# Operands of the blend in buffers of their own, loaded in the last gated block; loads of b on GpSimd's queue

## The chip, the cores and the metric

The kernel runs on one core of one Trainium2 chip. The metric is the device time of one execution in microseconds; the times given are medians over several executions, with the lowest and the highest beside them. All durations are read from one profiled execution of each kernel.

## What is computed

A linear attention with a decaying state feeds two feed-forward layers; every matrix product is in fp32.

```python
x = attention(q, k, v)                    # 3072 tokens x 512
a, b = x @ w1, x @ w2                     # 512 -> 1024, the "gated" products
h = a * b @ w3                            # 1024 -> 1024
x = h @ w_out                             # 1024 -> 512
h = x @ w_in                              # 512 -> 2048
g = h * (1 / (1 + exp(-1.702 * h)))
out = g @ w_out2                          # 2048 -> 512
```

The kernel multiplies `w3` by `w_out` once, on the chip, and calls the product the mixed weights, so `a * b` goes straight to 512 features.

## The kernel before, in words

TensorE multiplies in a reduced format, so each fp32 operand is **split** into a high part (ScalarE casts, `split` at L261) and a residue (DVE subtracts, `residue` at L162), and each product is made of three matmuls (`mm3`, L246 to L248: high by high, high weight by residue, residue weight by high). The order of the instructions on each engine is the order of the program; each engine waits in that order.

The stages are: attention, with preparation of weights in its gaps; **gated products** over six blocks of 512 tokens in the order 0, 2, 4, 1, 3, 5; **mixing**, the product of `w3` and `w_out`, which runs within the third of these blocks; the **blend**, which multiplies `a * b` by the mixed weights; then `Expand` and `contract` for the last layer.

From mixing on the products are made by a scheme of seven products in place of eight (P1 to P7 in the order of `blends`: P1, P5, P6, P2, P7, P3, P4) on pairs of blocks. Blocks 0, 2, 4 (`gate_first`) store `a * b` to the DRAM tensor `hd`. Blocks 1, 3, 5 (`gate_second`) load back what was stored (`load_b`, tile `h` of two buffers in pool `xs`) and form five further operands `g[:, 0:5]` from it: DVE and GpSimd subtract (L1021, L1024, L1025, L1026), and GpSimd stores the 1280 KB tile `g` into `hd` (L1027). Each block has eight gates (`t` from 0 to 7) of 24 matmuls in two PSUM banks out of six, and two gates make one `g`, so a block has four pairs `k`. A b tile is released by the sum L1026 that reads it last. In the last block `opening(t)` also loads the first mixed weights `wm` and the operand of turn 0 (`load_h`, L796).

The blend has 21 turns, seven products for each of three pairs of blocks. Turn `n` needs one operand of 1 MB from `hd` (tile `l`, four tags `l0` to `l3` by `n % 4`, 8 KB per partition each): it is loaded by SyncE, called SP here (`load_turn`, three turns ahead from turn 1 on), cast by ScalarE into a tile `h` of two buffers, and replaced by its residue on DVE (`split_h`), then multiplied in 24 matmuls with one of the mixed weights. P1, P5 and P6 are copied out of PSUM by ScalarE into tiles `s` (`copied`, L852); the turn's copies stand in the program behind the split of the next turn. A bank that holds P1 is accumulated on by P6 at turn 2.

Tiles live in pools. Pools on the left side of the on-chip memory are stacked in the order in which they are opened: `big` (weights of the gates), then `b1` (mixing; closed when the eight mixed rows are done), then `b2` (tiles `st`, `b12`, an unused `gap` of 4 KB, and two `g` of 10 KB), and, after the gated stage, `c` in the same place (the blend: `l2`, `l3`, `l0`, `l1`, then `o`, `h`, `s`). A pool's size is settled once the whole program is written, and a tag gets its place in the pool by its first request. With `reuse_waits="tile"` the first user of a tile waits until all earlier tiles that lay at that place have been read for the last time, stores to DRAM included. The operand of turn 1 is loaded in two halves into tiles of the pool `prep`, in the seventh gate of the last block (`t == KF - 2`); turns 2 and 3 are loaded at the start of `blend`, with three loads of `wm` between them.

Of the kernel before, what the change touches and what calls it, by code (L numbers as in the profile page):

```python
# [8 lines left out]
F32R = mybir.dt.float32r  # L9
# [7 lines left out]
P = 128  # L17
# [4 lines left out]
TB = 512  # L22
NB = NT // TB
CPB = TB // P
KD, KF, KG = DM // P, DF // P, DG // P
ALPHA = 1.702
R_BUFS = 5
# [10 lines left out]
NM = KF // 2  # L38
ORDER = (0, 2, 4, 1, 3, 5)
# [4 lines left out]
def tile_kernel(  # L44
# [14 lines left out]
    nc = tc.nc  # L59
    first, second, third = (ctx.enter_context(ExitStack()) for _ in range(3))  # L60
# [226 lines left out]
    def h_tile():  # L287
        return xs.tile([P, 2, TB], F32, tag="h", bufs=2, name="h")
# [504 lines left out]
    def load_h(n, a, b, t):  # L793
        i, name = blends[n]
        lo2.setdefault(n, []).append((a, b, t))
        nc.sync.dma_start(t.bitcast(F32), hd[i][:, a:b, RIGHT[name]])  # L796
# [13 lines left out]
    def split_wm(n):  # L810
        hi, lo = wm[blends[n][1]]
        split(hi, lo, lo.bitcast(F32))

    def load_wm(n):
        name = blends[n][1]
        wm[name] = wtile("wg")
        nc.sync.dma_start(wm[name][1].bitcast(F32), sm[PART[name]].rearrange("p k c -> p (k c)"))

    def opening(t):
        if t in range(1, 5):  # L820
            load_wm(t - 1)
        if t == 1:
            x = spare.tile([P, 7, TB], F32R, tag="ope", name="h0")
            hi2[0] = x[:, NM:]
            load_h(0, 0, NM, x[:, :NM])
        if t == KF - 2:
            for k in (0, 2):
                load_h(1, k, k + 2, prep.tile([P, 2, TB], F32R, tag="r", bufs=R_BUFS, name="h1"))
        if t in (3, 4, 5):
            split_h(0, t - 3, t - 2, hi2[0][:, t - 3 : t - 2])  # L830
        if t == 6:
            hi2["k3"] = prep.tile([P, TB], F32R, tag="x", bufs=6, name="h3")
            split_h(0, 3, 4, hi2["k3"].rearrange("p (a t) -> p a t", a=1))
        if t in (4, 6):
            split_wm(t // 2 - 2)

    def blend(p, ps, todo):
        ws = {}

        def tile(kind, bufs):  # L840
            return p.tile([P, NM, TB], F32R, tag=kind, bufs=bufs, name=kind)

        def load_turn(n):
            if n < len(blends):
                load_h(n, 0, NM, ls.pop(n) if n in ls else tile(f"l{n % 4}", 1))

        def value():
            return p.tile([P, TB], F32, tag="s", bufs=8, name="s")

        def copied(ps):  # L850
            t = ready.pop() if ready else value()
            nc.scalar.copy(t, ps)  # L852
            return t

        def store(i, e, t):
            nc.gpsimd.dma_start(yd[i][:, e], t)

        ls = {n: tile(f"l{n % 4}", 1) for n in range(2, 6)}
        load_turn(2)
        for n in range(4, 7):  # L860
            load_wm(n)
        load_turn(3)
        held = [p.tile([P, TB], F32, tag="o", bufs=2, name="c")]
        hi2[1] = tile("h", 2)
        ready = [value()]
        for n, (i, name) in enumerate(blends):
            if n < 7:
                ws[name] = [x.rearrange("p (k c) -> p k c", k=NM) for x in wm[name]]
            if n:
                load_turn(n + 3)  # L870
            if name == "P1":
                a, e, c = ([None] * 2 for _ in range(3))
                kept = [{}, {}]
            bank = dict(P5=e, P3=e, P2=c).get(name, a)
            for q in range(2):
                if name in ("P1", "P5", "P2"):
                    bank[q] = ps.tile([P, TB], F32, tag="m", bufs=8, name="m")
                for k in range(NM):
                    mm3(
                        bank[q],  # L880
                        *(x[:, k, q * P : (q + 1) * P] for x in ws[name]),
                        hi2["k3"] if (n, k) == (0, 3) else hi2[n][:, k],
                        low_h(n, k),
                        k == 0 and name in ("P1", "P5", "P2"),
                        k == NM - 1,
                    )
            if n == 7:
                left_tile(0)
                fetch_left(0)
            if n + 1 < len(blends):  # L890
                if n:
                    hi2[n + 1] = tile("h", 2)
                split_h(n + 1, 0, NM, hi2[n + 1])
            if n + 2 < 7:
                split_wm(n + 2)
            todo(n)
            for q, x in enumerate(kept):
                m = bank[q]
                if name in ("P1", "P5", "P6"):
                    x[name] = copied(m)  # L900
                if name == "P2":
                    nc.vector.tensor_tensor(x["P1"], m, x["P1"], ALU.add)
                    store(2 * i, q, x["P1"])
                if name == "P7":
                    nc.vector.tensor_tensor(x["P5"], m, x["P5"], ALU.add)
                    store(2 * i + 1, 2 + q, x["P5"])
                if name == "P3":
                    nc.vector.tensor_tensor(x["P6"], m, x["P6"], ALU.add)
                    store(2 * i + 1, q, x["P6"])
                if name == "P4":  # L910
                    t = held.pop() if held else p.tile([P, TB], F32, tag="o", bufs=2, name="c")
                    nc.scalar.copy(t, m)
                    store(2 * i, 2 + q, t)

    with tc.manual_schedule():
# [54 lines left out]
        with (  # L970
# [35 lines left out]

            hb = []

            def load_b(i, k):
                t = h_tile()  # L1010
                nc.sync.dma_start(t, hd[i // 2][:, k, :2])
                hb.append(t)

            def gate_second(t, i, ab):
                nonlocal b12, g
                b = hb[0]
                if t % 2 == 0:
                    b12 = first_b.pop() if first_b else b12_tile()
                    g = pb.tile([P, 5, TB], F32, tag="g", bufs=2, name="g")
                    gate_out(b12, ab)  # L1020
                    nc.vector.tensor_tensor(g[:, 1], b12, b[:, 0], ALU.subtract)  # L1021
                    return
                gate_out(g[:, 0], ab)
                nc.vector.tensor_tensor(g[:, 3], g[:, 0], b12, ALU.subtract)  # L1024
                nc.gpsimd.tensor_tensor(g[:, 2], g[:, 0], g[:, 1], ALU.subtract)  # L1025
                nc.gpsimd.tensor_tensor(g[:, 4], b[:, 1], g[:, 2], ALU.subtract)  # L1026
                nc.gpsimd.dma_start(hd[i // 2][:, t // 2, 2:], g)  # L1027
                hb.pop(0)

            def b12_tile():  # L1030
                return pb.tile([P, TB], F32, tag="b", bufs=2, name="b12")
# [2 lines left out]
            for n, i in list(enumerate(ORDER))[1:]:  # L1034
                nxt = ORDER[n + 1] if n + 1 < NB else None
                for t in range(KF):
                    if nxt is None:
                        opening(t)
                    elif t < 2:
                        for d in range(2):  # L1040
                            reload(nxt, 2 * t + d)
                    if n > 2 and t % 2 == 0 and t + 2 < KF:
                        load_b(i, t // 2 + 1)
                    if n >= 2 and nxt is not None and t == KF - 2:
                        load_b(nxt, 0)
                    ab = gate_mm(t, i, gate_tile)
                    if nxt is not None and t in range(KD - 1, KF - 1):
                        split_x(nxt, t - KD + 1)
                    work(((8, 6, 3, 3)[n - 1] + (n < 4) * (t % 2)) if n < 5 else (t < 4) + (t < 5))
                    (gate_second if n > 2 else gate_first)(t, i, ab)  # L1050
                    while rows < KF and (complete > W3 + rows or (n, t) == (2, KF - 1)):
                        ps = mix_mm(rows)
                        work(7)
                        mix_out(rows, ps)
                        rows += 1
                        if rows == KF:
                            stage.close()
                            pb = homes["st"] = stage.enter_context(
                                tc.tile_pool(name="b2", bufs=1, reuse_waits="tile")
                            )  # L1060
                            st_ready = [pb.tile([P, 1024], F32, tag="st", bufs=2, name="st")]
                            first_b = [b12_tile()]
                            pb.tile([P, 1024], F32, name="gap")
# [138 lines left out]
```

## Time and profile before

| | us |
|---|---|
| median of 3 runs (lowest to highest) | 981.96 (979.18 to 983.74) |
| span of the profiled execution | 982.2 |
| TensorE busy with matmuls | 963.9 |
| VectorE (DVE) busy | 718.7 |
| ScalarE (ACT) busy | 443.9 |
| GpSimd (POOL) busy | 203.3 |

The files show no time of the profiled execution beside its span. The busy shares come first: the engine that is busy nearly throughout sets the end, and what it waits for is where time can be won. The list of its waits tells which, the chain of work that ended last tells why, and the timeline of each engine around such a wait tells when each step ran. The granted clock is given for each stretch: 1.00 is 2.4 GHz and 0.50 is 1.2 GHz.

### The profile page before, as it was taken

Reading aid. Unit: us, or ns where it says so; the run is one execution under the profiler, and the core shown is the slowest. Engines: PE = TensorE matmul, PEld = TensorE weight load, DVE = VectorE, ACT = ScalarE, POOL = GpSimd, SP = SyncE. Lnnn points to the kernel's source line nnn. Section 1 sums busy time; section 2 is a strip of 40 time slices with the busy share of each in tenths; the row PEclk is TensorE's granted clock in tenths of the full one; section 3 lists DMA queues with packets and bytes.
Section 4 is the critical chain, followed back from the end, with each engine's and each line's share of the span. In section 5 each row is a group of like instructions: output and inputs, shape, how many; then the busy total and the mean of one; then the engine's idle time right before and its main releaser. Section 6 shows DMA issues by size and latency. Waiting matters only on the chain.

```text
span 982.2 us, 14858 instructions
## 1 busy us (share of the span) xinstructions
PE 963.9 (98%) x5608; PEld 835.2 (85%) x5608; DVE 718.7 (73%) x965; ACT 443.9 (45%) x787; POOL 203.3 (21%) x248
## 2 busy tenths in 40 slices
PE   7899999999999999999999999999999999999998
PEld 6788878888888888788889999999999888888886
DVE  4878878989898996765786895867777475567662
ACT  5666644443322222545536745444545544354430
POOL 5010000278685875250110000000000000000000
PEclk9999999999999999999999999999999999999999
DMA  9889965669998989979868647465596968767871
GB/s 362 347 325 355 354 208 192 220 232 346 319 318 324 347 316 356 402 254 322 269 233 296 242 176 278 174 235 223 202 360 253 331 227 282 244 192 251 288 236 54
DMA packets 115288, 268.73 MB, mean 274 GB/s; under 512 B 8000, under 2 KB 69440, under 8 KB 106128
## 3 DMA queue, kind: packets, MB, share of 16 engines
q1 hardware_dynamic: 100688, 193.98, 56.6%
q0 software_dynamic: 14384, 73.61, 19.2%
q8 instruction: 44, 0.72, 0.3%
q14 instruction: 28, 0.23, 0.1%
q10 hardware_dynamic: 144, 0.20, 0.1%
HBM read 165.52 MB, written 102.24 MB: 273 GB/s over the span
## 4 chain that ended last, share of the span: by engine, by line
PE 88%; DVE 5%; DMA 3%; ACT 2%; issue 1%; POOL 0%; DVEq 0%; ACTq 0%; POOLq 0%
PE m L247 11%; PE m L248 11%; PE m L246 11%; PE psm L246 7%; PE psm L247 7%; PE psm L248 7%; PE a L247 4%; PE a L248 4%; PE a L246 4%; PE e L248 2%; PE e L247 2%; PE e L246 2%; PE y L404 2%; PE s L354 2%; PE psg L246 1%
## 5 line engine op out<-in xcount | busy, mean ns | idle before, releaser
L246 PE MATMUL psm<-xh,wh 128*128 128x512 f32 x320 | 124.6, 389 | 0.0
L247 PE MATMUL psm<-xl,wh 128*128 128x512 f32 x320 | 124.5, 389 | 0.0
L248 PE MATMUL psm<-xh,wl 128*128 128x512 f32 x320 | 124.5, 389 | 0.0
L246 PE MATMUL m<-h,op 128*128 128x512 f32 x320 | 124.5, 389 | 0.0
L248 PE MATMUL m<-h,op 128*128 128x512 f32 x320 | 124.5, 389 | 0.0
L247 PE MATMUL m<-l,op 128*128 128x512 f32 x304 | 118.3, 389 | 0.0
L685 ACT CAST h<-l 128x2048 fp32r<-128x2048 f32 x38 | 72.3, 1914 | 83.0 <-PE m L248 58.0
L686 DVE TENSOR_TENSOR l<-l,h 128x2048 fp32r<-128x2048 f32 x38 | 85.6, 2286 | 20.7 <-ACT h L685 20.7
L247 PE MATMUL a<-yl,op 128*128 128x384 f32 x256 | 85.6, 334 | 0.1
L246 PE MATMUL a<-yh,op 128*128 128x384 f32 x256 | 85.6, 334 | 0.0
L248 PE MATMUL a<-yh,op 128*128 128x384 f32 x256 | 85.5, 334 | 0.0
L691 POOL DMA_DIRECT2D op<-sw x6 | 3.2, 533 | 393.2 <-PE a L248 212.9
L128 ACT ACTIVATE x<-raw 128x512 f32<-128x512 f32 x72 | 46.6, 672 | 76.1 <-DMA raw<-in_wo_dram 43.9
L246 PEld LDWEIGHTS psm<-xh,wh 128*128 128x128 f32 x320 | 60.1, 188 | 12.7 <-issue 0.2
L248 PEld LDWEIGHTS psm<-xh,wl 128*128 128x128 f32 x320 | 60.1, 188 | 12.5
L246 PEld LDWEIGHTS m<-h,op 128*128 128x128 f32 x320 | 60.1, 188 | 12.5
L248 PEld LDWEIGHTS m<-h,op 128*128 128x128 f32 x320 | 60.1, 188 | 12.4
L247 PEld LDWEIGHTS psm<-xl,wh 128*128 128x128 f32 x320 | 60.1, 188 | 12.3
L247 PEld LDWEIGHTS m<-l,op 128*128 128x128 f32 x304 | 57.1, 188 | 12.0
L246 PE MATMUL m<-h,wh 128*128 128x512 f32 x168 | 66.0, 393 | 0.6 <-ACT h L261 0.6
L248 PE MATMUL m<-h,wl 128*128 128x512 f32 x168 | 66.1, 393 | 0.0
L162 DVE TENSOR_TENSOR l<-l,h 128x2048 fp32r<-128x2048 f32 x19 | 43.5, 2291 | 29.8 <-ACT h L261 29.7
(165 smaller groups left out, 2209.3 us busy)
## 6 DMA issues: line engine op xcount, KB each, us to landing
gd<-g SPq DMA_DIRECT2D x32, 1344.0 KB, 4.7
qkv<-in_qkv_dram POOLq DMA_DIRECT2D x20, 1024.0 KB, 9.1
l<-gd SPq DMA_DIRECT2D x26, 768.0 KB, 6.9
l<-hd SPq DMA_DIRECT2D x19, 1024.0 KB, 7.8
raw<-in_w_dram SPq DMA_DIRECT2D x30, 512.0 KB, 5.1
hd<-g POOLq DMA_DIRECT2D x12, 1280.0 KB, 8.7
raw<-in_wo_dram SPq DMA_DIRECT2D x24, 512.0 KB, 7.5
l<-gd SPq DMA_DIRECT2D x24, 512.0 KB, 5.1
```

The costliest lines, as they stand in the source:

```text
L128: nc.scalar.activation(x, high, AF.Abs, scale=2.0**16)
L162: nc.vector.tensor_tensor(lo, x, hi.bitcast(F32), ALU.subtract)
L246: nc.tensor.matmul(ps, wh, xh, start=start, stop=False, skip_group_check=True)
L247: nc.tensor.matmul(ps, wh, xl, start=False, stop=False, skip_group_check=True)
L248: nc.tensor.matmul(ps, wl, xh, start=False, stop=stop, skip_group_check=True)
L354: nc.tensor.matmul(sc[c][j][:, p, :], qkt[c][r, 1, p, :], qkt[c][r, 0, p, :], start=True, stop=True,)
L404: nc.tensor.matmul(out_y, vs[c][:, 2 * p + j, :], pt[c][:, j, p, :], start=(p < 2), stop=first, skip_group_check=True,)
L685: nc.scalar.copy(hi, x.bitcast(F32))
L686: nc.vector.tensor_tensor(x, x.bitcast(F32), hi.bitcast(F32), ALU.subtract)
L691: queue.dma_start(t.bitcast(F32), sw[PART[name]])
```

## The change

The operands of turns 1, 2 and 3 get a pool `l` of 24 KB, opened when mixing ends, before `b2`, and kept open as long as `big`; they are loaded whole, all three at `t == 4` of the last gated block. `l0` stays in the blend's pool and is now its first tile. The loads of the mixed weights 4 to 6 go into gates 5 to 7 of the same block. `load_b` is issued by GpSimd, two pairs ahead, right behind the sums and the store of a pair; only the first two loads stay on SP.

```diff
--- before.py
+++ after.py
@@ -823,9 +823,11 @@
             x = spare.tile([P, 7, TB], F32R, tag="ope", name="h0")
             hi2[0] = x[:, NM:]
             load_h(0, 0, NM, x[:, :NM])
-        if t == KF - 2:
-            for k in (0, 2):
-                load_h(1, k, k + 2, prep.tile([P, 2, TB], F32R, tag="r", bufs=R_BUFS, name="h1"))
+        if t == 4:
+            for n in range(1, 4):
+                load_h(n, 0, NM, next_turn(n))
+        if t in range(5, 8):
+            load_wm(t - 1)
         if t in (3, 4, 5):
             split_h(0, t - 3, t - 2, hi2[0][:, t - 3 : t - 2])
         if t == 6:
@@ -834,6 +836,10 @@
         if t in (4, 6):
             split_wm(t // 2 - 2)
 
+    def next_turn(n):
+        home = homes["l0" if n % 4 == 0 else "l"]
+        return home.tile([P, NM, TB], F32R, tag=f"l{n % 4}", name="l")
+
     def blend(p, ps, todo):
         ws = {}
 
@@ -842,7 +848,7 @@
 
         def load_turn(n):
             if n < len(blends):
-                load_h(n, 0, NM, ls.pop(n) if n in ls else tile(f"l{n % 4}", 1))
+                load_h(n, 0, NM, first_l.pop() if n == 4 else next_turn(n))
 
         def value():
             return p.tile([P, TB], F32, tag="s", bufs=8, name="s")
@@ -855,11 +861,8 @@
         def store(i, e, t):
             nc.gpsimd.dma_start(yd[i][:, e], t)
 
-        ls = {n: tile(f"l{n % 4}", 1) for n in range(2, 6)}
-        load_turn(2)
-        for n in range(4, 7):
-            load_wm(n)
-        load_turn(3)
+        homes["l0"] = p
+        first_l = [next_turn(4)]
         held = [p.tile([P, TB], F32, tag="o", bufs=2, name="c")]
         hi2[1] = tile("h", 2)
         ready = [value()]
@@ -1006,10 +1009,12 @@
 
             hb = []
 
-            def load_b(i, k):
-                t = h_tile()
-                nc.sync.dma_start(t, hd[i // 2][:, k, :2])
-                hb.append(t)
+            def load_b(n, k, queue=nc.gpsimd):
+                n, k = n + k // NM, k % NM
+                if n < NB:
+                    t = h_tile()
+                    queue.dma_start(t, hd[ORDER[n] // 2][:, k, :2])
+                    hb.append(t)
 
             def gate_second(t, i, ab):
                 nonlocal b12, g
@@ -1026,6 +1031,7 @@
                 nc.gpsimd.tensor_tensor(g[:, 4], b[:, 1], g[:, 2], ALU.subtract)
                 nc.gpsimd.dma_start(hd[i // 2][:, t // 2, 2:], g)
                 hb.pop(0)
+                load_b(ORDER.index(i), t // 2 + 2)
 
             def b12_tile():
                 return pb.tile([P, TB], F32, tag="b", bufs=2, name="b12")
@@ -1039,10 +1045,10 @@
                     elif t < 2:
                         for d in range(2):
                             reload(nxt, 2 * t + d)
-                    if n > 2 and t % 2 == 0 and t + 2 < KF:
-                        load_b(i, t // 2 + 1)
-                    if n >= 2 and nxt is not None and t == KF - 2:
-                        load_b(nxt, 0)
+                    if n == 2 and t == KF - 2:
+                        load_b(n, NM, nc.sync)
+                    if n == 3 and t == 0:
+                        load_b(n, 1, nc.sync)
                     ab = gate_mm(t, i, gate_tile)
                     if nxt is not None and t in range(KD - 1, KF - 1):
                         split_x(nxt, t - KD + 1)
@@ -1055,6 +1061,9 @@
                         rows += 1
                         if rows == KF:
                             stage.close()
+                            homes["l"] = first.enter_context(
+                                tc.tile_pool(name="l", bufs=1, reuse_waits="tile")
+                            )
                             pb = homes["st"] = stage.enter_context(
                                 tc.tile_pool(name="b2", bufs=1, reuse_waits="tile")
                             )
```

## Rows read from the trace of the kernel before

**Rows 1.** The page, part 1: busy us, share of the span, instructions.
```profile
PE 963.9 (98%) x5608; PEld 835.2 (85%) x5608; DVE 718.7 (73%) x965; ACT 443.9 (45%) x787; POOL 203.3 (21%) x248
```
**Rows 2.** Waits of TensorE: who waited for whom, us in total, times, longest.
```profile
PE m L247 <- DVE l L162: 1.8, 1, 1.8
...
PE m L246 <- ACT h L261: 0.6, 1, 0.6
```
**Rows 3.** The chain that ended last, 398 to 417 us: start, us, what.
```profile
398.78 13.36 DMA l<-hd
```
**Rows 4.** Timeline of TensorE: start, us, engine, line, operation, out<-in, form, idle before.
```profile
397.06 0.39 PE L246 MATMUL m<-h,wh 128*128 128x512 f32 x1
...
402.50 0.39 PE L246 MATMUL m<-h,wh 128*128 128x512 f32 x1
...
413.16 0.39 PE L248 MATMUL m<-h,wl 128*128 128x512 f32 x1
...
416.50 0.69 PE L247 MATMUL m<-l,wh 128*128 128x512 f32 x1 [1.82 <-DVE l L162]
...
420.47 0.39 PE L248 MATMUL m<-h,wl 128*128 128x512 f32 x1
```
**Rows 5.** Stretches: length, busy us of each engine, granted clock, DMA share, GB/s.
```profile
416.00:418.00 2.00, 1.50 (x4) 1.21 (x5) 2.00 (x3) 2.00 (x3) 0.00 (x0) 0.66 1.03 388
418.00:420.00 2.00, 2.00 (x7) 1.51 (x6) 2.00 (x2) 0.78 (x1) 1.67 (x1) 0.50 0.12 45
```
**Rows 6.** Timeline of SP's queue around the end of the last gated block.
```profile
385.64 0.90 SPq L796 DMA_DIRECT2D h<-hd  x2
```
**Rows 7.** Stretches as in rows 5: PE, PEld, DVE, ACT, POOL, clock, DMA, GB/s.
```profile
360.00:370.00 10.00, 10.00 (x46) 8.29 (x45) 8.87 (x7) 2.29 (x4) 8.17 (x8) 1.00 0.76 260
...
380.00:390.00 10.00, 10.00 (x46) 8.29 (x45) 9.84 (x14) 5.22 (x9) 4.70 (x4) 1.00 0.82 282
...
402.00:411.00 9.00, 9.00 (x41) 7.44 (x41) 7.83 (x8) 4.42 (x5) 0.70 (x2) 1.00 1.02 406
```
**Rows 8.** Timelines of POOL, DVE and ACT, single instructions from 351 to 406 us.
```profile
351.01 0.56 POOL L1027 DMA_DIRECT2D hd<-g  x1 [0.30 <-POOL g L1026]
...
360.03 0.69 DVE L1021 TENSOR_TENSOR g<-b,h 128x512 f32<-128x512 f32 x1
...
379.00 0.62 ACT L261 CAST h<-h 128x512 fp32r<-128x512 f32 x1 [11.06 <-DMA h<-hd]
...
393.05 0.57 POOL L1027 DMA_DIRECT2D hd<-g  x1 [0.30 <-POOL g L1026]
...
402.43 0.57 POOL L1027 DMA_DIRECT2D hd<-g  x1 [0.30 <-POOL g L1026]
...
402.76 0.59 ACT L852 COPY s<-m 128x512 f32<-128x512 f32 x1 [2.19 <-PE m L248]
403.24 1.92 ACT L261 CAST h<-l 128x2048 fp32r<-128x2048 f32 x1
...
405.21 2.28 DVE L162 TENSOR_TENSOR l<-l,h 128x2048 fp32r<-128x2048 f32 x1
```
**Rows 9.** Waits of SP's queue, 340 to 420 us: us in total, times, longest.
```profile
SPq L1011 <- POOL g L1026: 34.7, 5, 10.8
SPq L796 <- DMA hd<-g: 10.9, 2, 6.3
SPq L796 <- DVE g L1024: 7.3, 1, 7.3
```
**Rows 10.** The twelve stores of `g`, then the last of them alone.
```profile
DMA to landing us min/median/max: 7.6/8.7/10.8
...
DMA to landing us min/median/max: 8.4/8.4/8.4
```
**Rows 11.** The page, part 6: DMA issues, count, KB each, median us to landing.
```profile
gd<-g SPq DMA_DIRECT2D x32, 1344.0 KB, 4.7
```
**Rows 12.** Line L148 from 270 to 276 us: three stores by GpSimd.
```profile
L148 POOL DMA_DIRECT2D sp<-x x2: 540/557/574, 272.6 to 273.1; - x2
...
L148 POOL DMA_DIRECT2D sp<-st x1: 537/537/537, 273.7 to 273.7; - x1
...
DMA to landing us min/median/max: 2.3/2.3/3.4
```

## Prediction

> **What bounds the kernel now.** I read the busy shares first: TensorE is busy for 963.9 us of a span of 982.2 us [rows 1], so a change can only win where TensorE stands still or runs slowly. Next I read what TensorE waited for [rows 2]: behind the attention part, the only waits of any size are two in the blend, 0.6 us for a cast `h` and 1.8 us for a residue `l`. Third, the chain around them [rows 3]: they belong to one event. The blend has begun at 397.06, but the load of one `l` tile starts only at 398.78 and takes 13.36 us; cast and residue follow, and TensorE has both at 416.50. Fourth, the matmuls themselves [rows 4]: a turn of the blend is 24 matmuls; turn 0 starts at 397.06 and turn 1 at 402.50, so one matmul is due every 5.44/24 = 0.2267 us, turn 2 at 407.94 and turn 3 at 413.38. The stall is therefore turn 3's (product P2). Fifth, the granted clock [rows 5]: 0.66 from 416 to 418 us and 0.50 (1.2 GHz) from 418 to 420, after TensorE had stood.
>
> So the stall costs more than its waits. From the matmul at 413.16 to the one at 420.47 there are 12 steps [rows 4]: 12 x 0.2267 = 2.72 us were due, 7.31 passed, **4.59 us are lost**. Of these 2.89 come before the second matmul of turn 3 (416.50, due 413.61), and 1.70 from the ten slow steps after it (3.97 for 2.27).
>
> **The change, part by part.**
>
> *Loads of turns 1 to 3.* They leave the end of SP's program (the first from 385.64 on, the last at 398.78 [rows 3, 6]) for the fifth gate of the last block, into tiles that overlie the first weight buffers of the mixing stage, long dead. SP has no wait in front of them there, so I expect them issued around 365 to 375 us. The same 3 MB are moved, earlier: 360 to 370 moved only 260 GB/s and 380 to 390 only 282, against 406 in a full stretch [rows 7], so there is room for about 10 x (0.41 - 0.26) + 10 x (0.41 - 0.28) = 2.8 MB. Turn 3's operand lands well before 413: gain 4.59 us, the upper bound of all that the change can bring. The loads of `wm` 4 to 6 also move forward; nothing waited for them, cost nothing either way.
>
> *Loads of b.* All but the first two leave SP for GpSimd's queue: ten more issues there. An issue of the same engine (`hd<-g`) takes 0.57 us [rows 8], so 5.7 us over some 120 us, on an engine that is not the bound (203.3 us busy in all [rows 1]). Each new issue stands behind its own pair's sums and store, so it never waits on GpSimd; queued behind it are the sums of the weight pieces and the next pair. SP loses its waits for the sums (34.7 us over five in this stretch alone [rows 9]), which is what lets the operands of turn 0 out earlier. Two buffers as before, released by the same sum, so a b load starts when it did. But it now follows a 1280 KB store in one queue. The store lands 7.6 to 10.8 us after issue [rows 10]. Lower bound: nothing; upper bound, taken from the longest store and 512 KB behind it at that store's rate (4.3 us): 15 us. The b that opens the last block would be issued behind the store of 351.01, near 351.6, and is read at 360.03 [rows 8]; with a store of 8.7 (the median) and about 2 us behind it, it lands near 362, some 2 us late. Cover: six PSUM banks, so TensorE needs a bank again only two gates (10.9 us) later. Cost on the path: 0; if the cover were used up, at most 15 - 10.9, about 4 us.
>
> *Where buffers now lie.* This decides. Pools are stacked in the order in which they are opened, and tags within a pool in the order of first request. In KB above `big`, before: `st` 0-8, `b` 8-12, the gap 12-16, `g` 16-36; over them in the blend `l2` 0-8, `l3` 8-16, `l0` 16-24, `l1` 24-32, `o` 32-36, `h` 36-52, `s` from 52. The waits fit that map: SP waits for L1024, the last reader of `b` (that is `l3`), and twice for a store `hd<-g` (that is `l0` and `l1` over `g`) [rows 9]. After: `l1` to `l3` 0-24, and the second gated pool above them, `st` 24-32, `b` 32-36, gap 36-40, `g` **40-60**; over these `l0` 24-32 and `o`, `h`, `s` where they were. So `l` is clear of `g`, but the first `h` (36-44) now lies on `g` buffer 0, the second `h` (44-52) and the first `s` (52-54) on `g` buffer 1 (50-60). What was a load's wait becomes ScalarE's: the cast of turn 1 waits for the store of pair 2, the copy of P1's first bank and the cast of turn 2 for the store of pair 3, the last. ScalarE runs in order: copy, copy, cast all stand behind that store, and TensorE needs the cast at turn 2.
>
> *Its price.* The last store is issued at 402.43 [rows 8], behind the sums L1025 and L1026, which need the last gated product; no edit moves that. It landed 8.4 us later, with DMA at 406 GB/s [rows 7, 10]. In the changed kernel most of the loads beside it are already through. Lower bound: a 1344 KB store from SP has a median of 4.7 [rows 11]. GpSimd's stores `sp` near 273 us took 2.3 us (128 KB each) and 3.4 (512 KB) [rows 12], which extended to 1280 KB gives 3.4 + 768 x 1.1/384 = 5.6. Upper bound 8.4, and 10.8 at the worst of the twelve [rows 10]. The loads of turns 3 and 4 and of `wm` 4 to 6, at most 3.5 MB, come forward across 402 us into room for 2.8, so up to 0.7 MB, or 1.7 us at 406 GB/s, may still be left there; sharing with part of that, I take 6.3, a little above the quiet value: landing 408.7. From there, by the pitch of the same instructions [rows 8]: from a copy to what follows it 403.24 - 402.76 = 0.48, twice; from cast to residue 405.21 - 403.24 = 1.97; the residue 2.28; and 0.10 for the hand-overs, together 5.31. Second matmul of turn 2 at 414.04, due 408.17: 5.87 us late. The slow clock afterwards: 1.70, the loss after the only such stall in the trace; bounds 0 (the clock holds) and 3.4 (turns 1 and 2 both pay). What turn 1 waits for pair 2's store is hidden: that store is issued at about 391 (ScalarE is no longer held 11.06 us by turn 0's load [rows 8]) or at the latest at 393.05 [rows 8], lands by 403.85 at the slowest rate of the twelve, and turn 1 then ends before 414 in most cases.
>
> Of this landing **the Trainium skill** (page "DMA: Bandwidth & Descriptors", section "Anatomy of one DMA") has a fit for DMAs from GpSimd's queue, 2.0 us plus bytes / 436e3; an estimate by it for 1.31 MB is 5.0 us. All twelve stores of this case took longer, 7.6 to 10.8. By the page's value the sum below would be 1.7 us and the time 983.6.
>
> **Sum** against the profiled execution, of which the files show the span, 982.2 us, and no time of its own: -4.59 + 5.87 + 1.70 = **+3.0 us**, 985.2. The span is 0.2 us above the median of the runs (981.96; they spread from 979.18 to 983.74), so I carry the difference over: **985.0 us**. With the store at 5.6 us the sum is +2.3, at 4.7 it is +1.4, at 8.4 it is +5.1.
>
> **The rivals.**
>
> *The new overlap does not bite* (the pools lie otherwise, or the first users of `h` and `s` do not wait for the store). Then only the gain is left: 981.96 - 4.59 = 977.4. Against it: the map above explains three waits of the trace one by one. For it: I derive the new map, no row shows it. Chance 0.15.
>
> *The last store lands as late as it did.* One mechanism: the pulled loads and the b loads have made a backlog, so the store shares its engines as before. It decides from a landing of 8.3 us on (sum +4.9). At 8.4 to 10.8 us the sum is +5.1 to +7.5: 987.0 to 989.5, I take 987.8. For it: the twelve stores never took under 7.6 [rows 10]. Against it: they all ran beside loads that are now earlier. Chance 0.22.
>
> The Trainium skill (page "SBUF — State Buffer", section "SBUF: two separate sides") holds that descriptors of GpSimd's DMAs are held up while VectorE runs certain fp32 operations, and advises against that queue. That would feed this rival. The trace does not show it: three stores' issues took 0.56 to 0.57 us [rows 8], with DVE busy 8.87 and 9.84 of 10 us in stretches beside them [rows 7].
>
> *b comes too late for the PSUM cover* in the last block, from about 11 us of delay on; then TensorE waits within the gates, about 4 us more: 989. The delay worked out above is 2 us. Chance 0.03.
>
> **How the numbers follow.** Forecast 0.60 (985.0, its own range 983 to 987), overlap harmless 0.15, late store 0.22, late b 0.03. A measurement of this kernel can tell about 0.5%, 4.9 us, from no change. The first two lie inside that except for the edges: the harmless case is at -4.6, and I give 0.4 of it to faster, 0.06 in all. Slower: most of the late store (0.17), late b (0.03) and the upper edge of the forecast (0.03), 0.23. Same: 0.71. The range: 983 to 987 holds 0.55; it is taken up to 988.5 for the late store, and down to 977.2 for about half of the harmless case, which leaves out under 0.2.
>
> **What would show it.** In the profile after: no wait of TensorE for turn 3; a wait for `h` and `l` at turn 2, behind a ScalarE copy `s<-m` or cast that waits for DMA `hd<-g`; a lowered clock right after it; SP issuing the `l` loads near 370 us; b loads in the rows of POOL's queue and no wait of SP for L1026. Wrong would be: ScalarE's first copy in the blend going through at 400 us as before, the last store landing outside 4.7 to 8.4 us, or a TensorE wait inside the last gated block.

## Result: 987.3 us after, against 981.9 before

| | before | after |
|---|---|---|
| median of 6 runs, us (lowest to highest) | 981.87 (979.18 to 984.20) | 987.32 (986.21 to 987.68) |
| span of the profiled execution, us | 982.2 | 985.5 |
| blend in the profile: its first matmul to the first of the next stage, us | 118.86 | 121.86 |

The time ratio is 1.0061, with an interval of 1.0044 to 1.0078: 0.6% slower. That is clear of no change, but the interval lies on both sides of 0.5%, which the prediction took for the least that a measurement of this kernel can tell. The profiled execution of after took 987.32 us, so 1.8 us lie outside its span; the same 1.8 us stand between time and span in every other execution that has both, to 0.1 us.

The busy shares and the waits of TensorE in the kernel after (the waits are: engine, line, what it waited for, us in total, times, longest):

```profile
PE 964.7 (98%) x5608; PEld 835.5 (85%) x5608; DVE 713.4 (72%) x964; ACT 444.3 (45%) x786; POOL 207.4 (21%) x258
```
```profile
PE m L247 <- DVE l L162: 3.6, 2, 1.8
PE m L246 <- ACT h L261: 1.2, 2, 1.0
```

Where before had one wait for a cast and one for a residue [rows 2], after has two of each: two stalls in place of one. The matmuls of the blend in the kernel after (start, us, engine and line, operation, tiles, shape; in brackets the idle time in front and what ended it) show where. The first row is the blend's first matmul and the last is the first of the next stage:

```profile
397.30 0.39 PE L246 MATMUL m<-h,wh 128*128 128x512 f32 x1
...
403.09 0.50 PE L246 MATMUL m<-h,wh 128*128 128x512 f32 x1 [0.18 <-ACT h L261]
405.42 0.50 PE L247 MATMUL m<-l,wh 128*128 128x512 f32 x1 [1.82 <-DVE l L162]
411.96 0.50 PE L246 MATMUL m<-h,wh 128*128 128x512 f32 x1 [1.00 <-ACT h L261]
414.29 0.64 PE L247 MATMUL m<-l,wh 128*128 128x512 f32 x1 [1.82 <-DVE l L162]
...
519.16 0.33 PE L246 MATMUL a<-yh,op 128*128 128x384 f32 x1
```

One matmul is due every 0.2267 us. The second matmul of turn 1 is the 26th, due at 397.30 + 25 x 0.2267 = 402.97; it came at 405.42, 2.45 us late. That of turn 2 is the 50th, due at 408.41; it came at 414.29, 5.88 us late, and this contains the first delay. Turn 3, which stalled before [rows 3, 4], waits for nothing. What holds turn 2 is in the chain around it (start, us, what):

```profile
401.82 7.12 DMA hd<-g
...
409.52 0.59 ACT s L858
410.11 1.81 ACT h L261
411.94 2.30 DVE l L162
414.29 0.64 PE m L247
```

and in ScalarE's timeline of the same stretch:

```profile
401.13 1.91 ACT L261 CAST h<-l 128x2048 fp32r<-128x2048 f32 x1 [5.71 <-DMA hd<-g]
...
409.04 1.07 ACT L858 COPY s<-m 128x512 f32<-128x512 f32 x2 [5.06 <-DMA hd<-g]
410.00 1.91 ACT L261 CAST h<-l 128x2048 fp32r<-128x2048 f32 x1
```

ScalarE twice waits for a **store** of `g`: its cast of turn 1 for the store of pair 2, its copy of the first bank of P1 for the last store. Behind that copy stands the cast that turn 2 needs. Then the clock falls (columns: stretch, its length, busy us and count of PE, PEld, DVE, ACT, POOL, granted clock, DMA share, GB/s):

```profile
406.00:408.00 2.00, 2.00 (x10) 1.65 (x9) 1.43 (x3) 0.00 (x0) 0.00 (x0) 1.00 0.44 184
...
414.00:416.00 2.00, 1.71 (x4) 1.33 (x5) 2.00 (x4) 2.00 (x2) 0.00 (x0) 0.62 0.66 255
416.00:418.00 2.00, 2.00 (x6) 1.60 (x5) 2.00 (x2) 0.57 (x1) 0.00 (x0) 0.52 0.00 0
```

After the first stall it stayed at 1.00, after the second it fell to 0.62 and 0.52, nearly down to 1.2 GHz.

### The profile page after: what moved, and what is told of

Same layout as the page of the kernel before. It is cut to its first block, busy times and chain, and to the rows that moved or that the text cites. A ratio compares the mean times of both kernels' runs of the same rounds, so it can differ in the third digit from the quotient of the medians.

```text
span 985.5 us, 14842 instructions
## 1 busy us (share of the span) xinstructions
PE 964.7 (98%) x5608; PEld 835.5 (85%) x5608; DVE 713.4 (72%) x964; ACT 444.3 (45%) x786; POOL 207.4 (21%) x258
## 4 chain that ended last, share of the span: by engine, by line
PE 55%; POOL 3%; DVE 3%; issue 2%; DMA 1%; ACT 1%; DVEq 0%; POOLq 0%; ACTq 0%
PE m L247 11%; PE m L248 11%; PE m L246 11%; PE a L247 4%; PE a L246 4%; PE a L248 4%; PE e L246 2%; PE e L247 2%; PE e L248 2%; PE c L246 1%; PE c L248 1%; PE c L247 1%; POOL g L1030 1%; POOL g L1031 1%; DMA hd<-g 1%
## 5 line engine op out<-in xcount | busy, mean ns | idle before, releaser
L686 DVE TENSOR_TENSOR l<-l,h 128x2048 fp32r<-128x2048 f32 x38 | 85.6, 2287 | 21.1 <-ACT h L685 21.0
L162 DVE TENSOR_TENSOR l<-l,h 128x2048 fp32r<-128x2048 f32 x20 | 45.8, 2292 | 36.5 <-ACT h L261 36.4
L247 PE MATMUL m<-l,wh 128*128 128x512 f32 x160 | 63.1, 394 | 3.6 <-DVE l L162 3.6
```

The source lines that it names most:

```text
L162: nc.vector.tensor_tensor(lo, x, hi.bitcast(F32), ALU.subtract)
L247: nc.tensor.matmul(ps, wh, xl, start=False, stop=False, skip_group_check=True)
L686: nc.vector.tensor_tensor(x, x.bitcast(F32), hi.bitcast(F32), ALU.subtract)
```

## Experiments

A yardstick for all of them: the time from the blend's first matmul to the first of the next stage, read from each profile's PE timeline as above. It is 114.24 us in each of the kernels whose blend has no wait of TensorE (e2_b_only, e4_clear, e5_clear2). The excess over that is what stalls cost, slow clock included.

| kernel | b on | blend's `h`, `s` | median us (ratio to before, interval) | profile's blend us | lost us | span, span less lost us |
|---|---|---|---|---|---|---|
| before | SP | clear of `g` | 981.87 | 118.86 | 4.62 | 982.2, 977.6 |
| after | GpSimd | over `g` | 987.32 (1.0061; 1.0044 to 1.0078) | 121.86 | 7.62 | 985.5, 977.9 |
| e1_before_again | SP | clear | 981.59 (0.9988; 0.9966 to 1.0011) | 119.67 | 5.43 | 984.0, 978.6 |
| e2_b_only | GpSimd | clear | 979.61 (0.9975; 0.9959 to 0.9991) | 114.24 | 0 | 978.7, 978.7 |
| e3_l_only | SP | over `g` | 991.17 (1.0095; 1.0068 to 1.0122) | 125.69 | 11.45 | 988.9, 977.5 |
| e4_clear | GpSimd | clear, `o` moved | 983.02 (1.0002; 0.9987 to 1.0018) | 114.24 | 0 | 980.2, 980.2 |
| e5_clear2 | GpSimd | clear | 979.70 (0.9969; 0.9954 to 0.9985) | 114.24 | 0 | 977.8, 977.8 |
| e6_sp_store | GpSimd | over `g` | 984.74 (1.0024; 1.0006 to 1.0041) | 119.61 | 5.37 | 983.6, 978.2 |
| e7_s_clear | GpSimd | `h` over `g` | 985.71 (1.0034; 1.0017 to 1.0052) | 119.86 | 5.62 | 984.1, 978.5 |
| e8_before_clear | SP | clear, `l3` too | 981.56 (0.9991; 0.9972 to 1.0010) | 116.39 | 2.15 | 979.2, 977.1 |
| e9_h_clear | GpSimd | `s` over last `g` | 988.71 (1.0062; 1.0039 to 1.0086) | 125.13 | 10.89 | 989.3, 978.4 |
| e10_l_clear | SP | clear | 983.92 (1.0027; 1.0012 to 1.0042) | 118.98 | 4.74 | 982.2, 977.5 |

The ratios of e1 to e10 compare with executions of before made beside each run: their medians are 982.59 us for e1 to e4 (29 executions), 981.69 for e5 to e8 (35) and 979.99 for e9 and e10 (21), which ran on another chip than e1 to e8. The medians of e9 and e10 are therefore set against the others with care; what their profiles lost is safer.

The last column is the reading to start with: but for e4, all spans less their loss lie within 977.1 and 978.7 us. The blend's stalls are nearly all in which these profiles differ.

Theory A, that of the prediction: in after, `h` and `s` lie where the last two `g` lay, so ScalarE waits for their stores. Its rivals: that the extra traffic or the later landing as such does it, and, for before, that turn 3 would stall wherever its tile lay.

**e1_before_again: how much of the time of before is its stall?** The kernel before, unchanged, in twelve more executions.

> The kernel before, unchanged, to see how far its own executions spread. Each execution of the changed kernel takes 1.8 us more than its span (987.32 against 985.5); by that the profiled execution of before, span 982.2, would have taken 984.0, 2.1 us above its median of 981.87. Theory A, the stall of turn 3 in before changes from execution to execution: ratio 1.000 +- 0.002, spans from 977 to 982.5, and in a profile with a shorter span the loss at turn 3 (matmul 83 of the blend against 83 x 0.2267 us) is smaller than the 4.59 us seen so far. Rival B, the spread lies elsewhere, as in the first loads of the attention: the loss at turn 3 is 4.6 us again, and the spans differ before 397 us.

They took 979.21 to 987.04 us: five within 979.2 and 979.9, three within 981.5 and 981.7, and 983.3, 985.6, 985.8 and 987.0. The profiled one (985.77 us) has the stall, with the load of turn 3 landing after 14.1 us. Its row of landing times, of ScalarE's cast and of the matmul that waited longest:

```profile
DMA to landing us min/median/max: 14.1/14.1/14.1
```
```profile
413.96 1.90 ACT L261 CAST h<-l 128x2048 fp32r<-128x2048 f32 x1 [4.26 <-DMA l<-hd]
...
418.24 0.50 PE L247 MATMUL m<-l,wh 128*128 128x512 f32 x1 [1.82 <-DVE l L162]
```

The median is as expected; the spans, 977.4 to 985.3 us, spread wider than the 977 to 982.5 expected, and no profile with a short span came of it, so it stays open whether the loss at turn 3 is smaller there. The two profiles of before differ by 1.8 us: 0.8 in the blend and 1.0 ahead of it (first matmul at 398.02 against 397.06), so not all of the spread is the stall.

The time of this profile less its loss is 985.77 - 5.43 = 980.3, near the lowest five; the profile of before gives 982.2 + 1.8 - 4.62 = 979.4. So the stall is probably not in every execution of before. No execution of the lowest group was profiled; that it runs without the stall is inferred from this sum, and from e2 and e5 below, which have no stall in the blend and spread over 1.7 and 1.9 us where this kernel spreads over 7.8. How many executions have the stall is not fixed either: beside e9 and e10 the median of before is 979.99, close to the kernels without a stall, with single executions up to 987.27.

**e2_b_only and e3_l_only: the two parts of the change, each alone.** The first is before with b on GpSimd, operands and layout as they were:

```diff
-            def load_b(i, k):
-                t = h_tile()
-                nc.sync.dma_start(t, hd[i // 2][:, k, :2])
+            def load_b(n, k, queue=nc.gpsimd):
+                n, k = n + k // NM, k % NM
+                if n < NB:
+                    t = h_tile()
+                    queue.dma_start(t, hd[ORDER[n] // 2][:, k, :2])
...
                 hb.pop(0)
+                load_b(ORDER.index(i), t // 2 + 2)
...
```

> The kernel before with only the loads of b moved to GpSimd, two pairs ahead; buffers and loads of the blend's operands stay. Theory A (the loss comes from ScalarE's waits for tiles that lie over g): no such tile here, so 982 +- 2 us, ratio 0.998 to 1.002, one stall at turn 3 as before. Rival B (b loads behind the stores in one queue cost time): 984 to 987 us, with TensorE or DVE waiting for b within the gates or the last store landing later than 8.4 us.

The second is after with these lines taken back.

> The changed kernel with the loads of b back on SP as in before; buffers and early loads stay. Theory A: the copy and the cast of ScalarE wait for the last store as in the changed kernel, 987 +- 1.5 us, ratio 1.004 to 1.007. Rival B: the loss belongs to the queue of b, so 979 to 982 us.

e2 took 979.61, faster than before, and has no stall at all, which neither theory had foreseen. SP's timeline in e2:

```profile
366.55 3.54 SPq L796 DMA_DIRECT2D h<-hd  x2
...
399.87 3.89 SPq L796 DMA_DIRECT2D l<-hd  x2
```

The halves of turn 1's operand are issued from 366.55 on, not from 385.64 [rows 6], since SP no longer stands in front of them until a sum has freed a tile of b. So they move in stretches that had room, ahead of the operands of turns 2 and 3 (issued at 387.83 and 399.87). The stretches of rows 7, in e2:

```profile
360.00:370.00 10.00, 10.00 (x46) 8.29 (x45) 9.87 (x11) 2.83 (x5) 9.51 (x10) 1.00 1.01 358
...
380.00:390.00 10.00, 10.00 (x46) 8.26 (x45) 9.84 (x14) 2.48 (x4) 5.48 (x5) 1.00 0.98 368
```

358 and 368 GB/s stand against 260 and 282 before [rows 7]. The load of turn 3 is issued at 399.87, no earlier than before (398.78), but lands after 6.8 us, where before took 13.36 [rows 3]:

```profile
DMA to landing us min/median/max: 6.8/6.8/6.8
```

e3 took 991.17, slower than after and beyond the 987 +- 1.5 of theory A: ScalarE waits as expected, but a second loss comes on top. Its DVE and PE timelines show why at the start of the blend:

```profile
400.04 0.69 DVE L1024 TENSOR_TENSOR g<-b,h 128x512 f32<-128x512 f32 x1 [6.35 <-DMA h<-hd]
```
```profile
401.38 0.50 PE L246 MATMUL m<-h,wh 128*128 128x512 f32 x1 [1.73 <-DVE g L285]
```

The last b was issued by SP at 384.46, behind three loads of 1 MB (from 370.28 on), and landed 15.5 us later; in after the same b, issued by GpSimd at 383.64, landed after 9.6. The sums and TensorE, which wants a bank back, wait for it, and the last store goes out at 404.89 (401.82 in after); then follow the stalls of turns 1 and 2 as in after. So the two parts pull in opposite ways, and the early operands need b out of their queue.

**e4_clear, e5_clear2: the layout alone.** After, with the tiles of the blend placed so that nothing that ScalarE writes early lies over `g`. In e4 the order of first requests in the blend changes, and the copies of P6 get a tag of their own:

```diff
...
+        hi2[1] = tile("h", 2)
         first_l = [next_turn(4)]
         held = [p.tile([P, TB], F32, tag="o", bufs=2, name="c")]
-        hi2[1] = tile("h", 2)
-        ready = [value()]
+        ready = {x: [value(x)] for x in "ts"}
...
-                    x[name] = copied(m)
+                    x[name] = copied(m, "t" if name == "P6" else "s")
```

> The changed kernel with the blend's tiles in another order, so that the two buffers of h lie at 24 to 40 KB, l0 at 40 to 48 (over the g whose store lands first), o at 48 to 52, the tiles of P6 at 52 to 60 and those of P1 and P5 at 60 to 68, clear of both g. Theory A: no stall at turns 1 and 2, none at turn 3, the granted clock 1.00 throughout; the 7.59 us that the changed kernel loses from matmul 0 to 59 of the blend are gone: 979.7 us, ratio 0.996 to 0.999 against before. Rival B: another wait takes the place (the operand of turn 4 over g, or the b queue), 983 to 987 us.

The blend lost nothing, as theory A said, but the kernel took 983.02, not 979.7: another wait took the place, as rival B said. The waits of TensorE and the timeline of ScalarE in e4:

```profile
PE a L246 <- ACT u L551: 2.5, 1, 2.5
```
```profile
521.63 0.48 ACT L551 COPY u<-a 128x384 f32<-128x384 f32 x1 [5.05 <-DMA yd<-c]
```

By the map, the tiles `o`, moved as well, now lay under one of the first copies of the next stage; the row shows it waiting for one of the blend's last stores (`yd<-c`). The same mechanism, made anew one stage later. e5 leaves `o` where after has it and moves `g` instead: it becomes the first tag of its pool (24 to 44 KB), the gap goes, and `h` and `s` come to lie from 44 KB on:

```diff
...
+                            first_g = [g_tile()]
                             st_ready = [pb.tile([P, 1024], F32, tag="st", bufs=2, name="st")]
                             first_b = [b12_tile()]
-                            pb.tile([P, 1024], F32, name="gap")
...
         held = [p.tile([P, TB], F32, tag="o", bufs=2, name="c")]
+        ready = {"t": [value("t")]}
         hi2[1] = tile("h", 2)
-        ready = [value()]
+        ready["s"] = [value("s")]
...
```

> The changed kernel with g placed first in the second gated pool (24 to 44 KB) and l0, o and the tiles of P6 over it, so that h (44 to 60) and the tiles of P1 and P5 (60 to 68) are clear of it, and o lies where it lay in the changed kernel, not under the first copies of the next stage as in the reordered kernel before. Theory A (waits for tiles that lie over stored ones are the whole loss): no stall in the blend nor behind it, 114.2 us from the blend's first matmul to the first of the next stage as with the b loads moved alone, 979.5 +- 0.7 us. Rival B (pulling 3 MB forward costs by itself): 981 us or more, with a wait for a load or for b.

979.70, as expected: no wait of TensorE in the blend, 0.4 us at the next stage's first copy, and a full clock (first line, the clock of the core; second, the waits of TensorE):

```profile
core 0: 977.8 us, clock 1.000
```
```profile
PE a L246 <- ACT u L551: 0.4, 1, 0.4
```

e5 keeps the early loads and b on GpSimd and takes away only the overlay, so the overlay is what made after slow: 987.32 - 979.70 = 7.6 us, and 7.62 us is what the profile of after lost in the blend.

**e6_sp_store and e7_s_clear: the price of the store.** In e6 the last store of `g` leaves by SP's queue; the waits stay.

```diff
-                nc.gpsimd.dma_start(hd[i // 2][:, t // 2, 2:], g)
+                queue = nc.sync if (i, t) == (ORDER[-1], KF - 1) else nc.gpsimd
+                queue.dma_start(hd[i // 2][:, t // 2, 2:], g)
```

> The changed kernel with the last store of g issued by SP, all else unchanged. Theory A: the stall of turn 2 follows the landing of that store one to one. Stores of this size from SP have a median of 4.7 us; landing 401.8 + 4.7 to 5.5 = 406.5 to 407.3 against 408.9, so second matmul of turn 2 near 412.2 against 414.3, 985.2 us (984.5 to 986.2). Rival B (ScalarE's order or the slow clock sets the loss, not the landing): 987 +- 0.5 us.

984.74, within what was expected, but by luck, not by the way expected. The store landed sooner:

```profile
DMA to landing us min/median/max: 5.9/5.9/5.9
```

and turn 2 did not wait at all, because turn 1 had already lost the time:

```profile
404.18 0.49 PE L246 MATMUL m<-h,wh 128*128 128x512 f32 x1 [1.36 <-ACT h L261]
406.51 0.50 PE L247 MATMUL m<-l,wh 128*128 128x512 f32 x1 [1.83 <-DVE l L162]
```
```profile
408.00:410.00 2.00, 2.00 (x6) 1.54 (x5) 0.53 (x1) 2.00 (x3) 0.00 (x0) 0.50 0.35 129
```

Turn 1 waits for the store of pair 2, 3.62 us late at its second matmul where after was 2.45 late, and this time the clock fell after it. So it is not shown that the stall of turn 2 follows the store one to one, as was expected. In e7 only the first tiles `s` are clear, P6's copies having a tag of their own below; `h` stays over `g`.

```diff
...
-        ready = [value()]
+        ready = {x: [value(x)] for x in "ts"}
...
-                    x[name] = copied(m)
+                    x[name] = copied(m, "t" if name == "P6" else "s")
```

> The changed kernel with only the tiles of the copies of P1 and P5 moved clear of g (60 to 68 KB); both h still lie over g. Theory A: the two copies go through near 400 and 403 us, but the cast of turn 2 waits for the same store; it starts 0.96 us sooner than behind the copies, so 986.4 us (985.8 to 987). Rival B, the copies alone are the cause: 980 to 983 us.

The copies no longer wait and the cast does:

```profile
404.45 1.06 ACT L858 COPY s<-m 128x512 f32<-128x512 f32 x2
...
410.11 1.91 ACT L261 CAST h<-l 128x2048 fp32r<-128x2048 f32 x1 [4.59 <-DMA hd<-g]
```

It took 985.71, a little under the 985.8 to 987 expected and far from the 980 to 983 of rival B. In the profiled execution the clock fell after turn 1 (0.50 from 408 to 410 us), inside time that turn 2 would have waited anyway, and not again: turn 2 came 5.45 us late, and 5.62 was lost in all.

**e8_before_clear: is it the place of `l3` that stalls before?** In before, the tile of turn 3 is put where nothing was read late, so that its load can be issued early.

```diff
-        ls = {n: tile(f"l{n % 4}", 1) for n in range(2, 6)}
+        ls = {n: tile(f"l{n % 4}", 1) for n in (2, 4, 5)}
+        held = [p.tile([P, TB], F32, tag="o", bufs=2, name="c")]
+        ready = {x: [value(x)] for x in "ts"}
+        ls[3] = tile("l3", 1)
+        hi2[1] = tile("h", 2)
...
```

> The kernel before, b loads on SP, with the blend's tiles in another order so that l3 lies at 44 to 52 KB, clear of everything: turn 3's load need not wait for the last reader of b12 and goes out right behind the loads of wm. Theory A: no stall at turn 3, 979.5 +- 0.7 us, and a spread of the runs of some 1.5 us like that with the b loads moved alone. Rival B: the load lands late anyway, from the backlog of SP's queue, 981.5 us or more with a spread of some 5 us.

The load was issued at 390.8, 8 us earlier than before, and landed at 410.9, where before had 398.78 + 13.36 = 412.14 [rows 3]; the rest of the head start went into a longer transfer:

```profile
DMA to landing us min/median/max: 20.1/20.1/20.1
```
```profile
415.27 0.50 PE L247 MATMUL m<-l,wh 128*128 128x512 f32 x1 [1.83 <-DVE l L162]
```

981.56 us (978.75 to 983.49), no different from before, as rival B said and against theory A's 979.5. Turn 3 still waits; here the clock held, so 2.15 us were lost. In before the transfers at the end of the stage are the limit, not the place of the tile. e2 has no such stall; that it is cured by moving bytes into stretches with room fits its rows, but was not tried by itself.

**e9_h_clear, e10_l_clear: e7 and e3 from the other side.** In e9, `g` is first in its pool as in e5, and the order in the blend puts the first `s` over the last `g` and both `h` clear of it.

```diff
         held = [p.tile([P, TB], F32, tag="o", bufs=2, name="c")]
-        hi2[1] = tile("h", 2)
         ready = [value()]
+        hi2[1] = tile("h", 2)
...
```

> The changed kernel with g first in the second gated pool, h clear of it (52 to 68 KB), but the first tile s still over the g that is stored last. Theory A: ScalarE runs in order, so the cast of turn 2 stands behind a copy that waits for that store although its own tile is free; turn 1 no longer waits, but what it waited was hidden: 987.3 +- 0.7 us, like the changed kernel. Rival B, only the tile that TensorE needs counts: 979.7 us.

988.71, far from rival B's 979.7: ScalarE's order counts, not only the tile that TensorE needs. Theory A expected 987.3 +- 0.7, like after, and missed by 1.4 us. The ten executions spread from 984.28 to 991.03, and the profiled one is the slowest of them, so its stall is not typical in size. In it the store was issued at 402.15, and SP had the load of `l0` out beside it at 401.52; the copy had to wait until 411.38:

```profile
411.38 1.07 ACT L858 COPY s<-m 128x512 f32<-128x512 f32 x2 [9.18 <-DMA hd<-g]
```
```profile
414.31 0.79 PE L246 MATMUL m<-h,wh 128*128 128x512 f32 x1 [4.75 <-ACT h L261]
```
```profile
418.00:420.00 2.00, 2.00 (x6) 1.53 (x5) 2.00 (x3) 0.92 (x1) 0.00 (x0) 0.50 0.00 0
```

TensorE stood once for 4.75 us; the clock was at 0.63 from 412 to 414 us and at 0.50 from 414 to 422. e10 is e5 with b on SP:

```diff
-            def load_b(n, k, queue=nc.gpsimd):
+            def load_b(i, k):
...
                 hb.pop(0)
-                load_b(ORDER.index(i), t // 2 + 2)
...
+                    if n > 2 and t % 2 == 0 and t + 2 < KF:
+                        load_b(i, t // 2 + 1)
...
```

> The kernel with no tile over a stored g (h at 44 to 60 KB, P1 and P5 at 60 to 68), with the loads of b back on SP. It parts the loss of the early loads with b on SP (11.4 us in the blend) into the wait over g and the wait for b. Theory A: b of the last pair stands behind the 3 MB of early loads in SP's queue, as it did there (DVE waited 6.35 us for it), so that TensorE waits about 1.7 us for a PSUM bank in turn 0: 115.9 to 117.7 us from the blend to the next stage, 981.4 to 983.1 us. Rival B, the late b costs nothing once ScalarE waits for no store: 979.7 +- 0.7 us.

983.92, beyond the 983.1 expected; the direction held. The late b alone, without the overlay, costs 4.74 us in its profile, by the same wait as in e3:

```profile
401.17 0.69 DVE L1025 TENSOR_TENSOR g<-b,h 128x512 f32<-128x512 f32 x1 [7.97 <-DMA h<-hd]
```
```profile
402.51 0.55 PE L246 MATMUL m<-h,wh 128*128 128x512 f32 x1 [2.83 <-DVE g L285]
```

That is 3.00 us until this matmul, the blend's 13th, and 1.74 in the slow clock behind it (0.50 from 404 to 406 us).

The losses do not add up: 4.74 here and 7.62 in after make 12.36, and e3, which has both causes, lost 11.45. There the wait for b cost 1.88 us and the clock held. Against after, e3 lost 3.83 us more: turn 2 came 8.55 us late and not 5.88, its store being issued 3.07 us later, and the slow clock cost 2.90 and not 1.74.

## Why the prediction came out as it did

**The stall of turn 3 goes: right.** The operands of turns 1 to 3 were issued from 365.74 us on (expected around 365 to 375), and turn 3 waits for nothing. SP's timeline in after:

```profile
365.74 10.32 SPq L796 DMA_DIRECT2D l<-hd  x3
```

**The overlap becomes ScalarE's wait: right.** The map of the buffers, worked out and seen in no row, was borne out by both waits for `hd<-g` and by e5, where moving the tiles alone takes them away. The place was right too: turn 2, with turn 1's own delay of 2.45 us lying inside that of turn 2.

**Its price: right, with two errors that cancelled.** Second matmul of turn 2: 5.88 us late (5.87 predicted); slow clock after it: 7.62 - 5.88 = 1.74 (1.70). Yet the store took 7.1 us and not 6.3, and was issued at 401.82, not at 402.43: 0.8 us more and 0.6 us less. The blend itself began 0.24 us later, at 397.30, and with it the time at which turn 2 was due. That these come to nothing is luck. The time of issue was held to be one that no edit moves; e3, at 404.89, moved it the other way. The rival of the late store, from 8.3 us on, did not occur.

The quiet value of 5.6 us, too, rests on a misreading: of the two stores that took 2.3 us one is of 256 KB, not 128. In before, from 270 to 276 us:

```profile
sp<-x POOLq DMA_DIRECT2D x1, 256.0 KB, 2.3
sp<-x POOLq DMA_DIRECT2D x1, 128.0 KB, 2.3
```

Extended from the larger one in the same way, the estimate is 3.4 + 768 x 1.1/256 = 6.7 us, nearer to the 7.1.

By the Trainium skill (page "DMA: Bandwidth & Descriptors", section "Anatomy of one DMA") the store would take an estimated 5.0 us; it measured 7.1 from GpSimd's queue, and 5.9 when e6 sent it from SP's. The measurement decides.

**The sum against the profile: right.** +3.0 us were predicted; the blend went from 118.86 to 121.86 us.

**From the profile to the median: the mis-sized term.** The gain, 4.59 us, was read from one execution of before that had the whole stall. It was then taken off the median, as if every execution had it. With the 1.8 us outside the span, the profiled execution of before took 982.2 + 1.8 = 984.0 us, near the slowest of the six (984.20). The prediction had set the span, 982.2, directly against the median, which carries these 1.8 us, and so took an execution with the whole stall for a typical one. The median of before is only 981.87 - 979.65 = 2.2 us above the kernels without a stall (979.61 and 979.70, mean 979.65). The change lost its 7.62 us against these: 979.65 + 7.62 = 987.3, which is what was measured. With 2.2 in place of 4.59, the prediction's own sum is -2.2 + 5.87 + 1.70 = +5.4, or 987.3 us. That term was 2.4 us too large. Because of it the time lies outside the 983 to 987 that the forecast of 985.0 gave itself; it is inside the stated range only because that was stretched to 988.5 for the late store, which did not occur. And the difference of the medians, 5.45 us, lies past the 4.9 us below which the prediction would say "same", its likeliest outcome (0.71), on the side to which it gave 0.23.

**b late: right that the PSUM banks cover it, too low in the delay.** The first b of the last block came in time, not 2 us late. The second, issued by GpSimd at 364.66, landed 11.9 us later, and DVE's sum waited for it 5.59 us; TensorE did not wait, since 5.59 is within the 10.9 us of cover:

```profile
376.65 0.69 DVE L1026 TENSOR_TENSOR g<-b,h 128x512 f32<-128x512 f32 x1 [5.59 <-DMA h<-hd]
```

GpSimd's ten issues of b took 0.53 to 0.75 us; the estimate was 0.57.

**What was missed: b on GpSimd is a gain by itself.** The prediction put it at nothing, and saw only that SP could send operands earlier. e2 shows 2.0 us (979.61 against 981.59 in e1, of the same chip; 2.5 us by its ratio). Its rows fit that very way: the two halves of turn 1's operand went out 19 us earlier, and the operand of turn 3 landed in 6.8 us. That the first brought the second is argued; the halves were not moved by themselves. The early loads of turns 2 and 3 added nothing to it (e5, 979.70).

## What to carry to other kernels

When a tile gets a home of its own, all tiles that were stacked above it move: draw up who lies over whom before and after, and for each tile ask whether its last reader is a store, and whether its next writer is a compute engine in order on the path; a load that waits for a buffer can be early, a copy cannot. Before moving loads ahead in a queue, look at what small, urgent load stands behind them (here 512 KB took 15.5 us behind 3 MB), and whether the engine that frees its buffer could issue it. A gain read from one profiled execution is worth only its share of the executions: set that execution's whole time against the median before adding it up.

## What the runs showed that was not expected

Stalls of the same look did not always cost the same. Standing 1.82 or 1.83 us for a residue, the clock then stayed at 1.00 in e8 and at turn 1 of after, and fell to 0.50 at turn 1 of e6 and of e7. Where it fell, some 1.7 us were lost again in before, after, e1, e6 and e10; in e3 and e9 it was 2.9 and 3.0, and in e9, after the longer standing (4.75 us), the clock stayed at 0.50 for 8 us. What decides between these is open; it was not tried by itself. It may be part of why the executions of before spread over 7.8 us, which is not shown.

A load that was issued 8 us earlier landed 1.2 us earlier (e8: 20.1 us for 1 MB). And a store's time to land was not a fixed price: the last one took 8.4 us in before [rows 10], 7.1 in after, 6.2 in e3 and 9.1 in e9, and the twelve stores of 1280 KB in after took 5.8 to 11.0 us each (7.6 to 10.8 before [rows 10]).
